# First wave of a fused attention-and-gMLP kernel: z2 of blocks 0 and 1 from centred x, the scale inside the gelu, the normed blocks through DMA transposes

## The chip, the cores and the metric

The kernel runs on one core of a Trainium2 chip. A core has a matrix engine (PE), a vector engine (DVE), an activation engine (ACT), a general engine (POOL) and a queue engine (SP) that here only issues DMAs. They run side by side and wait for each other through semaphores. The metric is device time in microseconds (us). Before the change it is 233.32 us, the median of 4 runs that lie between 233.18 and 233.46.

## The reference

x has 2048 rows (tokens) of 512 columns in bfloat16. The output is x, plus a dilated local attention of the normed x (A), plus a gated MLP of the normed x (B). Cut to what matters here:

```python
def _layernorm(x, axis=-1, eps=1e-05):
    m = jnp.mean(x, axis=axis, keepdims=True)
    v = jnp.var(x, axis=axis, keepdims=True)
    return (x - m) / jnp.sqrt(v + eps)
...
def _A_ref(x, wqkv, wo):              # 32 heads of 16, window 8, dilation 2
    qkv = ... x @ wqkv ...
    ...
    return (attention over 8 keys each) @ wo
def _B_ref(x, w_in, w_sp, b_sp, w_out):
    z = _gelu(jnp.einsum('bsd,df->bsf', x, w_in))     # 512 -> 1792
    z1 = z[..., :Fh].copy()                           # Fh = 896
    z2 = _layernorm(z[..., Fh:], axis=-1)
    g = jnp.einsum('ts,bsf->btf', w_sp, z2) + b_sp[None, :, None]
    return jnp.einsum('bsf,fd->bsd', z1 * g, w_out)
x = A_x
xn = _layernorm(x, axis=-1)
return x + _A_ref(xn, A_wqkv, A_wo) + _B_ref(xn, B_w_in, B_w_sp, B_b_sp, B_w_out)
```

## The kernel before

The 2048 rows are cut into 16 blocks of 128 rows. Everything is written as tasks with named inputs and outputs; a planner (`Plan`, L15) gives each engine one fixed order of its tasks before the program is built, from its own estimates, and puts in the semaphore waits. Some orders are written out by hand: `pe_seq` (most PE tasks stay in the order in which they are written), `dv` (the vector tasks of the first wave), a sequence of ACT tasks and one of SP loads (L734 to L739). When any task changes, the planner orders everything again, to the end of the kernel.

What happens, in order:

- **First wave** (`first_wave`, L659), blocks 0 to 3. Block b of x is loaded (L599). DVE takes its statistics (`bn`, L663) and mean and variance (`ag`, L667), POOL makes rstd, one over the root of the variance (L669), and DVE writes the normed block, (x - mean) * rstd (`nm`, L673). For block 0 this is done in two halves of 256 columns. PE transposes the block by four matmuls with the identity (`xt`, L682), ACT copies the transposed block out of PSUM into `xnT` (L688, and L700 for the two halves of block 0; DVE does it for block 3, L728). With `xnT` as the stationary operand PE multiplies by the second half of w_in (`z2_mm`, L911): per block two halves of 448 columns, each summed over four chunks dc of the 512 input columns, so 8 matmuls a block. For blocks 0 and 1 each half is cut in two tasks, chunks (0, 1) and chunks (2, 3). ACT writes gelu of the result to `z2`, with a running sum of it (L919).
- Before the first block is there, PE runs matmuls on constants (`warm`, 10 of 512 columns, L634), and one more (`fill0`) between the transposes of block 0 and block 1.
- **Wave j** (j = 0 to 3): Q and K of four blocks (L786), the products q*k on DVE (L812), their sums over a head on PE (L825, called red), V (L766), z2 of the next four blocks (L911), the layernorm of z2 (L952 squares, L958 to L974). From block 4 on the normed block does not go through PE: SP issues a DMA transpose from `xn` to `xnT` (L755).
- **z1** (L941), then the product with w_sp by a Strassen-like scheme of seven products (L1134), attention output (L1202, L1211), and the output product (L1253).

The w_in half for z2 is loaded in four chunks of 224 KB (L608): SP issues chunks 0 and 2, ACT chunks 1 and 3. Blocks 0 and 2 of x come from SP, blocks 1 and 3 from ACT. SP then issues Q weights and K weights (L620, 512 KB each), blocks 4 to 7 of x (L599), V weights (L627), blocks 8 to 11, and after these the DMA transposes of blocks 4 and up. x has eight slots; block 8 takes the slot of block 0.

The order on PE in the first wave is: warm; transposes of block 0, first half and second half; fill0; transposes of block 1; the z2 matmuls of chunks (0, 1) of blocks 0 and 1 (8 of them); chunks (2, 3) of block 0 (4); transposes of block 2; chunks (2, 3) of block 1 (4); transposes of block 3; z2 of blocks 2 and 3 (16); then Q and K of wave 0.

Of the kernel before, what the change touches and what calls it, by code (L numbers as in the profile page):

```python
# [14 lines left out]
class Plan:  # L15
# [287 lines left out]
BF = mybir.dt.bfloat16  # L303
F32 = mybir.dt.float32
ALU = mybir.AluOpType
# [9 lines left out]
    tmap=1,  # L315
    xdma=4,
    fill=1,
    warm=10,
    fill0=1,
    acc=1,  # L320
    first_plain=0,
# [3 lines left out]
def build_kernel(nc, A_x, A_wqkv, A_wo, B_x, B_w_in, B_w_sp, B_b_sp, B_w_out, out, report=False, sched_kw=None,  # L325
# [73 lines left out]
    with ExitStack() as es:  # L399
# [11 lines left out]
        def A(name, n, o2_=0):  # L411
            return ar[:, off[name] + o2_: off[name] + o2_ + n]
# [7 lines left out]
        def Fv(name, n, o2_=0):  # L420
            return fp[:, foff[name] + o2_: foff[name] + o2_ + n]
# [12 lines left out]
        def R1(key, name, n, o_=0):  # L434
            R(key, "sb", [(off[name] + o_, off[name] + o_ + n)])
# [24 lines left out]
        for s_ in range(4):  # L460
            R1(("xin", s_), "xin", 512, 512 * s_)
            if s_ < 2:
                R1(("xn0", s_), "xn", 256, 256 * s_)
            R1(("xin", 4 + s_), "xin2", 512, 512 * s_)
            R1(("xn", s_), "xn", 512, 512 * s_)
            R1(("Vn", s_), "Vn", 512, 512 * s_)
# [20 lines left out]
            R(("wk", c), "sb", [(off["wqk"] + 1024 * dc + 512 + 128 * c, off["wqk"] + 1024 * dc + 512 + 128 * c + 128)  # L487
                                for dc in range(4)])
        R1("wv_raw", "wv_raw", 2048)
        R("xnT0a", "sb", [(off["xnT"] + dc * S, off["xnT"] + dc * S + 128) for dc in range(2)])  # L490
        R("xnT0b", "sb", [(off["xnT"] + dc * S, off["xnT"] + dc * S + 128) for dc in range(2, 4)])
        for b in range(NB):
            R(("xnT", b), "sb", [(off["xnT"] + dc * S + 128 * b, off["xnT"] + dc * S + 128 * b + 128)
                                 for dc in range(4)])
# [30 lines left out]
        def T(eng, fn, **kw):  # L525
            t = plan.add(eng, fn, **kw)
            if eng == "pe" and not t.name.startswith(("warm", "fill", "xTr", "red")):
                pe_seq.append(t)
            return t
# [95 lines left out]
        for b in range(4, min(8, NB)):  # L625
# [1 line left out]
        dma("sp", lambda e: e.dma_start(A("wv_raw", 2048).rearrange("p (c n) -> p c n", c=4),  # L627
                                        A_wqkv[:, 1024:1536].rearrange("(c p) n -> p c n", p=128)),
            512 * 512 * 2, "wv", writes=["wv_raw"], name="ldwv")
        def filler(n, name, est, prio=None, reads=()):  # L630
            def warm(t):
                last = None
                for i in range(n):
                    last = t.matmul(ps[:, 3584: 4096], nc.const_aps.tensor(1.0, [128, 128], BF),  # L634
                                    nc.const_aps.tensor(1.0, [128, 512], BF), start=True, stop=True)
                return last
            T("pe", warm, reads=reads, writes=[("ps", 7)], est=est, name=name, prio=prio)

# [8 lines left out]
        def next_bank():  # L647
            k = ring[0]
            ring[0] = (k + 1) % NR
            return k  # L650
# [8 lines left out]
        def first_wave():  # L659
            dv = []  # L660

            def bn(b):
                dv.append(T("dve", lambda v: v.bn_stats(Fv("st6", 6, 9 * b), A("xin", 512, 512 * b)), reads=[("xin", b)],  # L663
                            writes=[("st6", b)], est=690, name="bnst%d" % b))

            def ag(b):
                dv.append(T("dve", lambda v: v.bn_aggr(Fv("mv", 2, 2 * b), Fv("st6", 9, 9 * b)), reads=[("st6", b), "st_eps"],  # L667
                            writes=[("mv", b)], est=200, name="bnag%d" % b))
                T("pool", lambda g: g.tensor_tensor(Fv("rstd", 1, b), Fv("mv", 1, 2 * b + 1), Fv("mhalf", 1), ALU.pow),  # L669
                  reads=[("mv", b), "mhalf"], writes=[("rstd", b)], est=580, name="rstd%d" % b)  # L670

            def nm(b, c0=0, n=512, wr=None, tag=""):
                dv.append(T("dve", lambda v: v.tensor_scalar(A("xn", n, 512 * b + c0), A("xin", n, 512 * b + c0), Fv("mv", 1, 2 * b),  # L673
                                                             Fv("rstd", 1, b), ALU.subtract, ALU.mult),
                            reads=[("xin", b), ("mv", b), ("rstd", b)],
                            writes=[wr or ("xn", b)], est=150 + n / 2, name="norm%d%s" % (b, tag)))

            def xt(b, k, dcs, rd, tag=""):
                def tr(t):
                    last = None  # L680
                    for dc in dcs:
                        last = t.matmul(ps[:, 512 * k + 128 * dc: 512 * k + 128 * dc + 128],  # L682
                                        A("xn", 128, 512 * b + 128 * dc), ident, start=True, stop=True)
                    return last
                T("pe", tr, reads=[rd, "ident"], writes=[("ps", k)], est=len(dcs) * c_mm(128), name="xt%d%s" % (b, tag))

            def ev(b, k):
                T("act", lambda a: a.activation(AC(off["xnT"] + 128 * b, [[S, 4], [1, 128]]),  # L688
                                                bank(k).rearrange("p (c n) -> p c n", c=4), ACTF.Copy),
                  reads=[("ps", k)], writes=[("xnT", b)], est=c_act(512), name="xTe%d" % b)  # L690

            bn(0)
            ag(0)
            bn(1)
            ag(1)
            k0, k1 = next_bank(), next_bank()
            for h in range(2):
                nm(0, 256 * h, 256, ("xn0", h), "ab"[h])
                xt(0, (k0, k1)[h], (2 * h, 2 * h + 1), ("xn0", h), "ab"[h])
                T("act", (lambda h: lambda a: a.activation(  # L700
                    AC(off["xnT"] + 2 * S * h, [[S, 2], [1, 128]]),
                    ps[:, 512 * (k0, k1)[h] + 256 * h: 512 * (k0, k1)[h] + 256 * h + 256].rearrange("p (c n) -> p c n", c=2),
                    ACTF.Copy))(h),
                  reads=[("ps", (k0, k1)[h])], writes=["xnT0" + "ab"[h]], est=c_act(256), name="xTe0" + "ab"[h])
            filler(cfg["fill0"], "fill0", 216.0 * cfg["fill0"], reads=(("xn0", 1),))
            nm(1)
            k = next_bank()
            xt(1, k, range(4), ("xn", 1))
            ev(1, k)
            bn(2)  # L710
            ag(2)
            bn(3)
            nm(2)
            ag(3)
            nm(3)
            u = [(b, hf, next_bank()) for b in range(2) for hf in range(2)]
            for b, hf, k in u:
                z2_mm(b, hf, k, (0, 1))
            for b, hf, k in u:
                if b == 1 and hf == 0:  # L720
                    k2 = next_bank()
                    xt(2, k2, range(4), ("xn", 2))
                    ev(2, k2)
                z2_mm(b, hf, k, (2, 3))
                z2_gelu(b, hf, k)
            k = next_bank()
            xt(3, k, range(4), ("xn", 3))
            dv.append(T("dve", (lambda k: lambda v: v.tensor_copy(  # L728
                AC(off["xnT"] + 128 * 3, [[S, 4], [1, 128]]), bank(k).rearrange("p (c n) -> p c n", c=4)))(k),
                reads=[("ps", k)], writes=[("xnT", 3)], est=c_dve(512), name="xTe3"))  # L730
            for b in (2, 3):
                z2_half(b, 0)
                z2_half(b, 1)
            plan.sequence(dv)  # L734
            sq = {t.name: t for t in plan.tasks if t.name.startswith("ld")}
            plan.sequence([sq[n] for n in ("ldq", "ldk", "ldx4", "ldx5", "ldx6", "ldx7", "ldwv")])
            names = ["xTe0a", "xTe0b", "xTe1", "z2g0_0", "xTe2", "z2g0_1", "z2g1_0"]
            named = {t.name: t for t in plan.tasks if t.name in names}
            plan.sequence([named[n] for n in names])  # L739
# [167 lines left out]
        def z2_mm(b, hf, k, dcs=range(4)):  # L907
            def mm(t):
                last = None
                for dc in dcs:  # L910
                    last = t.matmul(ps[:, 512 * k: 512 * k + HF], AC(off["xnT"] + dc * S + 128 * b, [[1, 128]]),  # L911
                                    AC(off["w_in2"] + FH * dc + HF * hf, [[1, HF]]), start=(dc == 0), stop=(dc == 3))
                return last
            rd = "xnT0" + "ab"[dcs[0] // 2] if b == 0 else ("xnT", b)
            T("pe", mm, reads=[rd] + [("w_in2", dc) for dc in dcs], writes=[("ps", k)],
              est=len(dcs) * c_mm(HF), name="z2_%d_%d_%d" % (b, hf, dcs[0]))

        def z2_gelu(b, hf, k):
            T("act", lambda a: a.activation(  # L919
                A("z2", HF, FH * b + HF * hf), ps[:, 512 * k: 512 * k + HF], ACTF.Gelu_apprx_tanh,  # L920
                accum_out=Fv("s1", 1, 2 * b + hf)),
              reads=[("ps", k)], writes=[("z2h", b, hf), ("s1", b, hf)], est=c_act(HF, accum=True),
              name="z2g%d_%d" % (b, hf), tbl="gelu")

        def z2_half(b, hf):
# [475 lines left out]
```

## Time and profile before

| what | value |
|---|---|
| median of 4 runs | 233.32 us (233.18 to 233.46) |
| the profiled execution | 233.59 us, of it a span of 231.7 us |
| PE busy | 226.7 us of the span |
| DVE busy | 205.0 us |
| ACT busy | 128.6 us |
| POOL busy | 40.8 us |
| DMA queue of SP (q1) | 59.1% of 16 DMA engines' time |

The span runs from the first to the last instruction; the 1.9 us around it are start and end of the execution. Clock times below (such as "at 8.02") are us from the start of the span. Busy PE time is modelled for the end of each matmul, so start-to-start distances are used for its pace. A few matmul records are missing from the trace.

### The profile page before, as it was taken

Reading aid. Unit: us, or ns where it says so; the run is one execution under the profiler, and the core shown is the slowest. Engines: PE = TensorE matmul, PEld = TensorE weight load, DVE = VectorE, ACT = ScalarE, POOL = GpSimd, SP = SyncE. Lnnn points to the kernel's source line nnn. Section 1 sums busy time; section 2 is a strip of 40 time slices with the busy share of each in tenths; the row PEclk is TensorE's granted clock in tenths of the full one; section 3 lists DMA queues with packets and bytes.
Section 4 is the critical chain, followed back from the end, with each engine's and each line's share of the span. In section 5 each row is a group of like instructions: output and inputs, shape, how many; then the busy total and the mean of one; then the engine's idle time right before and its main releaser. Section 6 shows DMA issues by size and latency. Waiting matters only on the chain.

```text
span 231.7 us, 3288 instructions
## 1 busy us (share of the span) xinstructions
PE 226.7 (98%) x1222; PEld 111.6 (48%) x1238; DVE 205.0 (88%) x235; ACT 128.6 (56%) x235; POOL 40.8 (18%) x74
## 2 busy tenths in 40 slices
PE   8999999999999999999999999999999999999995
PEld 2444445444434565555555454454545444545442
DVE  4688996998998899999999999999999999979910
ACT  2698758975899997556562243333423433255321
POOL 4456838197007101000000000000000000000000
DMA  6974999783107300449609999999999647745162
GB/s 201 336 213 100 206 269 317 129 250 117 34 16 166 106 3 0 99 82 219 215 9 185 235 208 250 254 214 256 278 314 180 166 167 139 260 103 112 44 151 68
DMA packets 76800, 38.65 MB, mean 167 GB/s; under 512 B 65132, under 2 KB 75244, under 8 KB 75760
## 3 DMA queue, kind: packets, MB, share of 16 engines
q1 hardware_dynamic: 70400, 31.63, 59.1%
q10 hardware_dynamic: 5568, 4.69, 7.1%
q0 software_dynamic: 816, 2.12, 3.0%
q8 instruction: 10, 0.16, 0.3%
q14 instruction: 6, 0.05, 0.1%
HBM read 18.49 MB, written 4.21 MB: 98 GB/s over the span
## 4 chain that ended last, share of the span: by engine, by line
PE 94%; DMA 3%; issue 1%; ACTq 1%; DVE 0%; ACT 0%
PE ps L1134 37%; PE ps L1253 16%; PE ps L786 12%; PE ps L941 11%; PE ps L911 10%; PE ps L766 6%; PE ps L825 3%; DMA arena<-in_A_x_dram 3%; ACTq L608 0%; PE ps L682 0%; DVE fpool L663 0%; ACTq L599 0%; DVE arena L673 0%; ACT arena L1095 0%
## 5 line engine op out<-in xcount | busy, mean ns | idle before, releaser
L1134 PE MATMUL ps<-arena 128*128 128x448 bf16 x448 | 90.6, 352 | 0.0
L1134 PEld LDWEIGHTS ps<-arena 128*128 128x128 bf16 x448 | 43.8, 98 | 42.8 <-ACT arena L1095 0.3
L1253 PE MATMUL ps<-arena 128*128 128x512 bf16 (+2 forms) x178 | 42.1, 366 | 0.5
L1202 DVE TENSOR_TENSOR arena<-arena 128x4096 bf16<-128x4096 bf16 x16 | 36.6, 2287 | 0.2
L812 DVE TENSOR_TENSOR arena<-arena 128x4096 bf16<-128x4096 bf16 x16 | 36.3, 2281 | 0.0
L1211 DVE TENSOR_TENSOR arena<-arena 128x4096 bf16<-128x4096 bf16 (+2 forms) x24 | 33.7, 1402 | 1.1 <-DMA arena<-arena 0.3
L1095 ACT ACTIVATE arena<-ps 128x512 bf16<-128x512 f32 (+2 forms) x23 | 13.0, 564 | 34.4 <-PE ps L1134 24.0
L786 PE MATMUL ps<-arena 128*128 128x512 bf16 x124 | 27.9, 379 | 0.3 <-issue 0.2
L1253 PEld LDWEIGHTS ps<-arena 128*128 128x128 bf16 x187 | 17.9, 98 | 18.5
L911 PE MATMUL ps<-arena 128*128 128x448 bf16 x128 | 25.5, 353 | 0.0
L941 PE MATMUL ps<-arena 128*128 128x448 bf16 x128 | 24.8, 353 | 0.0
L1027 DVE TENSOR_TENSOR arena<-arena 128x1024 bf16<-128x1024 bf16 x32 | 21.0, 686 | 0.9 <-DMA arena<-in_B_w_sp_dram 0.6
L919 ACT ACTIVATE arena<-ps 128x448 bf16<-128x448 f32 x32 | 17.2, 547 | 4.8 <-PE ps L911 2.9
L786 PEld LDWEIGHTS ps<-arena 128*128 128x128 bf16 x128 | 12.3, 98 | 15.5 <-issue 1.3
L941 PEld LDWEIGHTS ps<-arena 128*128 128x128 bf16 x128 | 14.4, 114 | 10.2 <-issue 0.8
L947 ACT ACTIVATE arena<-ps 128x896 bf16<-128x896 f32 x16 | 14.4, 916 | 8.7 <-PE ps L941 8.7
L794 ACT ACTIVATE arena<-ps 128x1024 bf16<-128x1024 f32 x16 | 16.3, 1019 | 4.8 <-PE ps L786 4.3
L911 PEld LDWEIGHTS ps<-arena 128*128 128x128 bf16 x128 | 12.2, 98 | 11.7 <-issue 0.4
L952 ACT ACTIVATE arena<-arena 128x896 bf16<-128x896 bf16 x16 | 15.1, 945 | 0.1
L766 PE MATMUL ps<-arena 128*128 128x512 bf16 x61 | 14.1, 379 | 0.4 <-issue 0.3
L1143 ACT ACTIVATE ps<-ps,fpool 128x448 f32<-128x448 f32 x16 | 9.7, 605 | 8.2 <-PE ps L1134 8.2
L1095 ACT ACTIVATE ps<-arena 128x512 f32<-128x512 bf16 (+2 forms) x17 | 9.7, 574 | 6.4 <-ACT arena L1095 4.7
(70 smaller groups left out, 196.2 us busy)
## 6 DMA issues: line engine op xcount, KB each, us to landing
arena<-vscr SPq DMA_DIRECT2D x8, 1152.0 KB, 6.4
arena<-in_A_x_dram ACTq DMA_DIRECT2D x18, 128.0 KB, 4.1
vscr<-arena POOLq DMA_DIRECT2D x16, 128.0 KB, 3.5
arena<-in_A_x_dram SPq DMA_DIRECT2D x14, 128.0 KB, 5.4
out_dram<-arena ACTq DMA_DIRECT2D x14, 128.0 KB, 2.6
arena<-in_A_wqkv_dram SPq DMA_DIRECT2D x3, 512.0 KB, 6.2
arena<-in_B_w_in_dram SPq DMA_DIRECT2D x1, 896.0 KB, 5.0
arena<-in_B_w_out_dram SPq DMA_DIRECT2D x1, 896.0 KB, 6.2
```

The source lines that it names most:

```text
L766: last = t.matmul(bank(k), AC(off["xnT"] + dc * S + 128 * b, [[1, 128]]), AC(off["wv_raw"] + 512 * dc, [[1, 512]]), start=(dc == 0), stop= ...
L786: last = t.matmul(bank(k + which), AC(off["wqk"] + 1024 * dc + col0, [[1, 128]]), AC(off["xnT"] + dc * S + 512 * j, [[1, 512]]), start=(dc ...
L812: T("dve", lambda v: v.tensor_tensor(pbv, qb, kb, ALU.mult), reads=rd, writes=[("pb", s_)], est=c_dve(4096, 2.0), name="prod%d_%d" % (j, c ...
L911: last = t.matmul(ps[:, 512 * k: 512 * k + HF], AC(off["xnT"] + dc * S + 128 * b, [[1, 128]]), AC(off["w_in2"] + FH * dc + HF * hf, [[1, H ...
L919: T("act", lambda a: a.activation(A("z2", HF, FH * b + HF * hf), ps[:, 512 * k: 512 * k + HF], ACTF.Gelu_apprx_tanh, accum_out=Fv("s1", 1, ...
L941: last = t.matmul(ps[:, 512 * (k + hf): 512 * (k + hf) + HF], AC(off["xnT"] + dc * S + t0, [[ts, 128]]), AC(off["w_in1"] + FH * dc + HF * ...
L1027: T("dve", (lambda o_, x_, y_: lambda v: v.tensor_tensor(o_, x_, y_, ALU.subtract))(o_, x_, y_), reads=rd, writes=[wr], est=c_dve(NK * 128 ...
L1095: T("act", lambda a: a.activation(out_, in_, ACTF.Copy), reads=reads, writes=writes, est=c_act(n), name=name)
L1134: last = t.matmul(half(bk), lh(k), rh(k), start=(new and k == 0), stop=(k == NK - 1), skip_group_check=True)
L1202: T("dve", (lambda tv, iv, av: lambda v: v.tensor_tensor(tv, iv, av, ALU.mult))(tv, iv, av), reads=[("attn", j)] + ([("Ve", par)] if q < 2 ...
L1211: T("dve", (lambda o_, n: lambda v: v.tensor_tensor(o_, two(0, n), two(n, n), ALU.add))(o_, n), reads=[] if n > 512 else ["Vs", ("Ve", par ...
L1253: last = t.matmul(po, lh, rh, start=False, stop=(q == len(order) - 1), skip_group_check=True)
```

## The change

In words:

- For blocks 0 and 1 DVE writes x - mean (`ce`, without rstd) to a scratch place in `pb`, block 0 in two halves. PE transposes these centred blocks, ACT copies them to a new place `XCT`, and the z2 matmuls of blocks 0 and 1 read that place. The factor rstd, one number a row, is given to the gelu of these two blocks as its scale.
- The normed blocks 0 and 1 are still needed for Q, K, V and z1. DVE writes them as before (`nm`, now whole blocks), after the centred ones, and SP issues a DMA transpose for each (`xd`) into `xnT`.
- SP's order becomes: Q weights, K weights, transpose of block 0, block 8 of x, transpose of block 1, blocks 4 to 7, V weights, blocks 9 to 11, transposes of block 4 and up (with block 12 ahead of the transpose of block 7).
- `warm` goes from 10 to 8 matmuls, `fill0` from 512 to 256 columns.
- The statistics of block 1 follow the centring of block 0. DVE's order in the first wave becomes: statistics 0, centre 0 (two halves), statistics 1, centre 1, norm 0, statistics 2, norm 1, statistics 3 and norm 2, norm 3.
- PE's order in the first wave becomes: warm; transposes of block 0 (two halves); fill0; block 0, first half of columns, chunks (0, 1) (2 matmuls); transposes of block 1; block 0, second half, chunks (0, 1) (2); block 0, first half, chunks (2, 3) (2); block 1, chunks (0, 1) (4); block 0, second half, chunks (2, 3) (2); transposes of block 2; block 1, chunks (2, 3) (4); transposes of block 3; z2 of blocks 2 and 3; Q and K.
- The planner's new order further on differs in places: statistics of block 8 stand ahead of those of block 4 on DVE; each group of reds stands one PE task later than before (the first one three tasks later); the product of wave 3, pair 1 stands behind the softmax subtraction of wave 2 and the z2 layernorm of wave 3 on DVE.

The diff, cut to its core:

```diff
-    warm=10,
+    warm=8,
...
+        R1("xc1", "pb", 512, 512)
+        XCT = off["pb"] + 1024
...
+            def ce(b, c0, n, wr, tag=""):
+                dv.append(T("dve", lambda v: v.tensor_scalar(A("pb", n, 512 * b + c0), A("xin", n, 512 * b + c0),
+                                                             Fv("mv", 1, 2 * b), None, ALU.subtract),
+                            reads=[("xin", b), ("mv", b)], writes=[wr], est=150 + n / 2, name="cent%d%s" % (b, tag)))
+
+            def xd(b):
+                dma("sp", lambda e: e.dma_start_transpose(AC(off["xnT"] + 128 * b, [[S, 4], [1, 128]]),
+                                                          A("xn", 512, 512 * b)),
+                    128 * 512 * 2, ("xT", b), reads=[("xn", b)], writes=[("xnT", b)], name="xTd%d" % b, xbar=True)
...
             bn(0)
             ag(0)
+            k0, k1 = next_bank(), next_bank()
+            for h in range(2):
+                ce(0, 256 * h, 256, ("xc0", h), "ab"[h])
+                xt(0, (k0, k1)[h], (2 * h, 2 * h + 1), ("xc0", h), "ab"[h])
...
+            filler(cfg["fill0"], "fill0", 216.0 * cfg["fill0"], reads=(("xc0", 1),), w=256)
             bn(1)
             ag(1)
...
+            ce(1, 0, 512, "xc1")
+            nm(0)
             bn(2)
             ag(2)
+            nm(1)
             bn(3)
             nm(2)
             ag(3)
             nm(3)
+            for b in range(2):
+                xd(b)
+            kx = next_bank()
             u = [(b, hf, next_bank()) for b in range(2) for hf in range(2)]
...
+            z2_mm(*u[0], (0, 1))
+            xt(1, kx, range(4), "xc1")
...
+            z2_mm(*u[1], (0, 1))
+            z2_mm(*u[0], (2, 3))
+            z2_gelu(*u[0])
+            z2_mm(*u[2], (0, 1))
+            z2_mm(*u[3], (0, 1))
+            z2_mm(*u[1], (2, 3))
+            z2_gelu(*u[1])
+            k2 = next_bank()
+            xt(2, k2, range(4), ("xn", 2))
+            ev(2, k2)
+            for b, hf, k in u[2:]:
                 z2_mm(b, hf, k, (2, 3))
                 z2_gelu(b, hf, k)
...
-            plan.sequence([sq[n] for n in ("ldq", "ldk", "ldx4", "ldx5", "ldx6", "ldx7", "ldwv")])
+            plan.sequence([sq[n] for n in ("ldq", "ldk", "xTd0", "xTd1", "ldx4", "ldx5", "ldx6", "ldx7", "ldwv")])
...
+                    xo = XCT + dc * 256 + 128 * b if b < 2 else off["xnT"] + dc * S + 128 * b
+                    last = t.matmul(ps[:, 512 * k: 512 * k + HF], AC(xo, [[1, 128]]),
                                     AC(off["w_in2"] + FH * dc + HF * hf, [[1, HF]]), start=(dc == 0), stop=(dc == 3))
...
             T("act", lambda a: a.activation(
                 A("z2", HF, FH * b + HF * hf), ps[:, 512 * k: 512 * k + HF], ACTF.Gelu_apprx_tanh,
+                scale=Fv("rstd", 1, b) if b < 2 else 1.0,
                 accum_out=Fv("s1", 1, 2 * b + hf)),
```

## The prediction

> **What bounds the kernel now.** I read the page first, then the chain that ended last in order of time, then the timelines of PE, DVE and SP over the first 24 us.
>
> ```profile
> span 231.7 us, 3288 instructions
> ...
> PE 226.7 (98%) x1222; PEld 111.6 (48%) x1238; DVE 205.0 (88%) x235; ACT 128.6 (56%) x235; POOL 40.8 (18%) x74
> ...
> PE 94%; DMA 3%; issue 1%; ACTq 1%; DVE 0%; ACT 0%
> ```
>
> PE is the bound: 98% busy and 94% of the chain. The rest of the chain is DMA, and the chain in order of time shows which:
>
> ```profile
> 2.21 5.95 DMA arena<-in_A_x_dram
> 8.16 0.02 issue
> 8.19 0.69 DVE fpool L663
> 8.88 0.32 DVE arena L673
> 9.21 0.05 issue
> 9.25 0.40 PE ps L682 x4
> 9.65 0.76 PE ps L911 x4
> 10.41 0.03 issue
> 10.43 0.40 PE ps L682 x4
> 10.83 3.03 PE ps L911 x16
> ```
>
> The load issued at 2.21 on ACT is block 3 of x. It lands at 8.16; its statistics, norm and transposes follow, and from 10.43 on PE never stands still: over 14 to 215 us the list of PE's waits holds 0.5 us, all "issue" beside missing records. So the end of the kernel is 10.43 plus PE work that the change leaves as it is. The PE timeline up to there:
>
> ```profile
> 5.49 0.57 PE L682 MATMUL ps<-arena 128*128 128x128 bf16 x4 [0.22 <-DVE arena L673]
> 5.90 0.38 PE L634 MATMUL ps<-const-bfloat16-1.0 128*128 128x512 bf16 x1
> 6.36 0.40 PE L682 MATMUL ps<-arena 128*128 128x128 bf16 x4
> 6.59 2.54 PE L911 MATMUL ps<-arena 128*128 128x448 bf16 x12
> 9.25 0.40 PE L682 MATMUL ps<-arena 128*128 128x128 bf16 x4
> 9.49 0.92 PE L911 MATMUL ps<-arena 128*128 128x448 bf16 x4
> 10.43 0.40 PE L682 MATMUL ps<-arena 128*128 128x128 bf16 x4
> ```
>
> Read starts, since ends are modelled. A z2 matmul takes 0.19 us (0.76 / 4 in the chain), four transposes 0.24 (10.43 to 10.67). Twelve z2 matmuls from 6.59, with a stop of 0.1 at 7.35 for the copy of block 1 (ACT 6.79 + 0.60), end at 8.97; PE then idles 0.28 until the norm of block 2 lets it go at 9.25, and 0.19 more before 10.43. PE is already early here: it waits for DVE, and DVE for x:
>
> ```profile
> 6.99 0.69 DVE L663 BATCH_NORM_STATS2 fpool<-arena 128x6 f32<-128x512 bf16 x1 [0.69 <-DMA arena<-in_A_x_dram]
> 8.19 0.69 DVE L663 BATCH_NORM_STATS2 fpool<-arena 128x6 f32<-128x512 bf16 x1 [0.27 <-DMA arena<-in_A_x_dram]
> 9.96 0.41 DVE L673 TENSOR_SCALAR arena<-arena,fpool 128x512 bf16<-128x512 bf16 x1 [0.66 <-POOL fpool L669]
> ```
>
> **The start of block 0.** Statistics 0 end at 4.40. Norm 0 started at 5.11, behind statistics 1 and rstd 0; the centring needs neither and starts at about 4.44, so the first transpose moves from 5.49 to 4.44 + 0.38 = 4.82, 0.67 earlier. Subtracting alone is not in the trace; the nearest rows, the norm of 256 columns (0.33) and of 512 (0.41), price it, and nothing at all below. Two constant matmuls fewer (each 0.42: the ten end at 5.27) end the warm-up at about 4.4, so they don't delay it.
>
> **Where the 0.67 goes.** Block 1 is centred behind centre 0 and statistics 1: 4.44 + 0.58 (two halves) + 0.65 + 0.2 give 5.9 with the hand-overs, where norm 1 stood before (5.89). Its transposes stay at 6.36, its copy at 7.39. Until then PE has four z2 matmuls of block 0, done by 7.0. The next in its order are chunks (2, 3) of block 0, which need chunk 2 of w_in: issued at 2.18 and 5.8 to landing in the DMA view, 7.97. Before, PE filled this time with block 1 and came to these chunks at 8.02, just after the landing. Now it idles from 7.0 to 8.02 and has 2 + 4 + 2 = 8 matmuls ahead of the transposes of block 2, not 4: 8.02 + 8 x 0.19 = 9.54 (norm 2 is ready at 9.21), + 0.24 + 4 x 0.19 = 10.54 for the transposes of block 3, against 10.43. The whole gain is lost in the wait for w_in, and **0.1 us** is added. The bound below is 0: norm 3 is done at 9.96 + 0.41 = 10.37, tied to a load whose rivals in the queues do not change before 8.16. Above: PE before could take 0.47 (0.28 + 0.19) of a later w_in chunk, and now none, so a chunk 0.3 later would cost 0.4.
>
> **Norms 0 and 1 on DVE**, 2 x 0.41, fall into its waits for x: norm 0 at 6.2 to 6.65, before 6.99; norm 1 at 7.83 (after the mean of block 2, 7.72 + 0.11), the next instruction 0.33 later at 8.16, before 8.19. Cost 0; if statistics 3 slipped, norm 3 and PE would slip by as much. rstd 0 and 1 on POOL are done by 6.5, before either use.
>
> **The gelu with a row scale** (4 of 32): without scale L919 takes 0.54; with a per-row operand, the L1143 copies of the same size take 0.605. 4 x 0.06 at most on ACT, which at 11.6 and later stays over 0.5 us ahead of the PE tasks that reuse its PSUM banks. Cost 0.
>
> **SP, with all that it now issues.**
>
> ```profile
> 5.45 1.99 SPq L599 DMA_DIRECT2D arena<-in_A_x_dram  x4
> 7.48 0.48 SPq L627 DMA_DIRECT2D arena<-in_A_wqkv_dram  x1
> 13.76 9.15 SPq L755 DMA_TRANSPOSE arena<-arena  x7
> ```
>
> Transpose 0 waits on SP for norm 0 (6.7), and a transpose takes SP 1.27; then block 8 (0.45), transpose 1 from 8.4 to 9.7, blocks 4 to 7 from 9.7 (before 5.45), V weights 11.7, blocks 9 to 11, transposes of block 4 on. The queue moves in order: K weights, issued at 4.90, land 6.2 later at 11.1; blocks 4 to 7 then came 0.37 apart (11.5 to 12.6). A transpose moves as many bytes as such a load, 0.37, or takes at most what is left of its quiet 2.5 to landing after 1.27 of issue, 1.2. So transpose 1 lands between 11.1 + 3 x 0.37 = 12.2 and 11.1 + 1.2 + 0.37 + 1.2 = 13.9. Q of wave 0 needs it at 13.7 + 0.1 = 13.8. I take the middle, 13.0: no stall, hidden behind the z2 matmuls of blocks 2 and 3; past them each us costs one. Four transposes issued from 31.64 to 41 behind larger loads took 7.2 to 11.3 to landing: that would be 15.6 to 19.7, 1.8 to 5.9 late. They stood behind 2.3 MB and beside POOL's stores, and nothing like it runs at 11 us, so those rows are far.
>
> Blocks 4 to 7 land at 13.1 to 14.3, 1.6 later; the transpose of block 7, issued at 17.70 before, goes out near 19.6 and lands near 22, and Q of wave 1 starts at 24.1. V weights land near 15.7 and are used at 20.6. Covered by 2 us and more; with that gone, PE would wait for DVE's norms.
>
> **DVE further on** starts wave 1 1.5 late and has 0.7 more work. Its waits take that up: 0.94 at 72.67, 0.58 at 76.36 (for w_sp), over 2 us between 33 and 42. Its tightest hand-overs to PE were 0.6 to 0.8 us (softmax subtraction, 91.70 + 1.22, to the reds at 93.51; the product at 99.15 + 2.28 to 102.18), and those reds now stand one z1 group (0.76) later. Cost 0; if 1.5 came through whole, 1.5 - 0.7 = 0.8.
>
> **Sum.** +0.1 on 231.7, 231.8; on the profiled 233.59, 233.7. That execution is 0.27 above the median, so the median goes from 233.32 to **233.4**.
>
> **The clock, bounded from rows.** PE starts at half pace: constant matmuls 0.42 apart for 512 columns, later 0.216. The windows' granted clock says 1.00 throughout, so only the distances show it. Full pace came between 5.06 and 5.49, 4.2 to 4.65 after the first matmul, in unbroken work. Now PE rests 0.4 to 0.6 us before 4.82, 0.25 before 5.75 and up to 1 us before 8.02. If a rest restarts the count, full pace comes at 4.82 + 4.65 = 9.5 or 8.02 + 4.65 = 12.7, and the half-pace work after 8.02 costs (9.5 - 8.02) / 2 = 0.7 to 4.65 / 2 = 2.3. I take 0: in the stretch that ended in full pace before, part of a rest of 0.4 may already have lain.
>
> The Trainium skill speaks against the change here: "TensorE: Matmul & The Clock Gate", Part 1, says that full clock needs a busy window of about 3.4 us whose phase is not tied to the kernel. Eight constant matmuls at 0.42 are 3.4 us, so by that page hardly any phase leaves a window without a rest; were windows with a rest refused, each would cost half of 3.4, an estimate of 1.7 us. No row here shows how much rest a window bears.
>
> **Rivals.**
> - *The clock stays low* (PE, 4.8 to 12.7): for it the new rests, against it the four runs before, 0.28 us apart. 0.7 to 2.3, middle 1.5: **234.9**. It decides once half pace lasts beyond 8.02.
> - *Q of wave 0 waits for transpose 1*: decides from a landing after 13.8, each us is one us; with 15.6, **235.2**.
> - *DVE comes late to the reds* at 94 to 103: 0.8, **234.2**.
> - *The early start is carried to the end*, as it would be were PE bound by its own work from 5.49: 233.32 - 0.67 = **232.65**. PE's 98% speaks for it, the chain through the load of x against it.
>
> **How the numbers follow.** Forecast 0.52, clock 0.17, transposes 0.11, DVE 0.10, early start 0.10. Faster or slower is told from no change at 0.2%, 0.47 us. Same: 0.47 of the forecast and 0.01 of the transposes, 0.48. Slower: 0.05 + 0.17 + 0.10 + 0.10 = 0.42. Faster: 0.10. The forecast's own range is 233.2 to 233.8. For 8 in 10 the range must reach over most of the clock's and transposes' cases: 232.9 to 235.5 leaves out the early start and about 0.08 above.
>
> **What would show it.** First transposes at 4.8; PE idle from 7.0 to 8.0; transposes of block 3 at 10.5; Q at 13.8 without a wait; no PE waits later. Wrong if z2 matmuls after 8.02 are 0.37 apart (clock), if Q starts after 14, if L825 waits for DVE, or if the transposes of block 3 start before 10.3.

## The result, and the profile after

The changed kernel takes 233.74 us, the median of 37 executions (233.12 to 235.98); the kernel before, timed beside it, 233.25 us (56 executions, 232.82 to 233.83). The ratio is 1.0027, with a 95% interval of 1.0019 to 1.0035: slower by half a microsecond in the median and by 0.63 in the mean (233.91 against 233.28), which the ratio follows; that is a little more than the 0.2% that can be told from no change. Beside the median the upper end has moved: 8 of the 37 executions lie above 234.2, none of the 56 before.

The profiled execution took 233.8 us, with a span of 231.18 (231.74 before). Its 2.62 us around the span are unusual; the other profiled executions of this study have 1.84 to 2.01. Span, busy time and the chain, from the page of the kernel after:

```profile
span 231.2 us, 3295 instructions
...
PE 225.4 (98%) x1220; PEld 111.4 (48%) x1236; DVE 206.4 (89%) x237; ACT 129.1 (56%) x235; POOL 40.2 (17%) x74
...
PE 95%; DMA 2%; issue 1%; SPq 1%; ACT 0%
```

The chain of the kernel after in order of time (start, us, what):

```profile
2.18 5.03 DMA arena<-in_B_w_in_dram
7.21 0.05 issue
7.26 1.69 PE ps L935 x8
8.95 0.22 PE ps L694 x4
9.17 0.76 PE ps L935 x4
9.93 0.22 PE ps L694 x4
10.15 3.03 PE ps L935 x16
```

The load in the chain is no longer block 3 of x but chunk 2 of w_in, issued at 2.18 on SP, landed at 7.21. From there PE is bound by itself: eight z2 matmuls, transposes of block 2, four matmuls, transposes of block 3. The PE timeline of the kernel after:

```profile
0.84 3.57 PE L637 MATMUL ps<-const-bfloat16-1.0 128*128 128x512 bf16 x8 [0.84 <-PEq L1411]
4.49 0.48 PE L694 MATMUL ps<-arena 128*128 128x128 bf16 x4
4.80 0.27 PE L637 MATMUL ps<-const-bfloat16-1.0 128*128 128x256 bf16 x1
5.75 0.54 PE L935 MATMUL ps<-arena 128*128 128x448 bf16 x2 [0.67 <-DMA arena<-in_B_w_in_dram]
6.12 0.39 PE L694 MATMUL ps<-arena 128*128 128x128 bf16 x4
6.34 0.54 PE L935 MATMUL ps<-arena 128*128 128x448 bf16 x2
7.26 1.69 PE L935 MATMUL ps<-arena 128*128 128x448 bf16 x8 [0.37 <-DMA arena<-in_B_w_in_dram]
...
9.76 0.39 PE L694 MATMUL ps<-arena 128*128 128x128 bf16 x4
```

The transposes of block 0 start 1.00 earlier than before (4.49, not 5.49; 0.28 of it because block 0 landed earlier, at 3.16 and not 3.44), yet PE gives it back in two waits for w_in, chunk 1 (landed 5.61) and chunk 2. The time from chunk 2's matmuls to the transposes of block 3, 9.76 - 7.26 = 2.50, is what matters: the prediction had 2.52.

That the transposes of block 3 start at 9.76 here and at 10.43 in the profile before is no gain of the change. In this execution the loads happened to land early: block 3 at 7.41, before at 8.16. With the loads of the execution before (chunk 2 at 7.96) the same work gives 7.96 + 0.05 + 2.50 = 10.51.

Two sums help to read all that follows. From the transposes of block 3 to the last matmul PE takes 218.7 us before (229.13 - 10.43 = 218.70) and after (228.45 - 9.76 = 218.69), and the span ends 221.3 us (before) or 221.4 us (after) behind these transposes. So an execution's span tells when its block 3 was transposed, unless PE waits later. Over all executions the median span is 231.3 before (35 executions of one batch) and 231.8 after (37), which is 10.0 and 10.4 for the transposes of block 3.

The wait for chunk 2 alone does not explain this. Chunk 2 and block 3 land together: in the twelve profiled executions that keep the order of the first loads, chunk 2 came 0.17 to 0.26 ahead of block 3. By the old chain the transposes of block 3 start 2.27 behind the landing of block 3 (10.43 - 8.16). In the four profiled executions in which PE takes up chunk 2 within 0.14 of its landing and at full pace, they start 2.29 to 2.45 behind it (the profile after 9.76 - 7.41 = 2.35, twelve constants 2.29, and the two runs with the K weights moved 2.43 and 2.45). So in executions like these the new chain costs 0.02 to 0.18 over the old, however late the two loads come. The rest of the half microsecond must lie in the pace of PE or in a later wait, unless the first loads land later with the change; the profiles do not show that they do (block 3 at 7.11 to 8.10 with it, 7.42 to 8.16 without).

### The profile page after: what moved, and what is told of

It reads as the page before. It is cut to its first block, busy times and chain, and to the rows that moved or that the text cites. A ratio compares the mean times of both kernels' runs of the same rounds, so it can differ in the third digit from the quotient of the medians.

```text
span 231.2 us, 3295 instructions
## 1 busy us (share of the span) xinstructions
PE 225.4 (98%) x1220; PEld 111.4 (48%) x1236; DVE 206.4 (89%) x237; ACT 129.1 (56%) x235; POOL 40.2 (17%) x74
## 4 chain that ended last, share of the span: by engine, by line
PE 95%; DMA 2%; issue 1%; SPq 1%; ACT 0%
PE ps L1159 37%; PE ps L1278 16%; PE ps L809 12%; PE ps L966 11%; PE ps L935 10%; PE ps L789 6%; PE ps L848 3%; DMA arena<-in_B_w_in_dram 2%; SPq L602 0%; PE ps L694 0%; SPq L611 0%; ACT arena L1120 0%
## 5 line engine op out<-in xcount | busy, mean ns | idle before, releaser
L835 DVE TENSOR_TENSOR arena<-arena 128x4096 bf16<-128x4096 bf16 x16 | 36.2, 2280 | 0.0
L809 PE MATMUL ps<-arena 128*128 128x512 bf16 x124 | 27.9, 379 | 0.3 <-issue 0.2
L809 PEld LDWEIGHTS ps<-arena 128*128 128x128 bf16 x128 | 12.4, 98 | 15.3 <-issue 0.4
L943 ACT ACTIVATE arena<-ps 128x448 bf16<-128x448 f32 x28 | 15.1, 548 | 2.0
L789 PE MATMUL ps<-arena 128*128 128x512 bf16 x61 | 14.7, 379 | 0.3 <-issue 0.2
```

The costliest lines, as they stand in the source:

```text
L789: last = t.matmul(bank(k), AC(off["xnT"] + dc * S + 128 * b, [[1, 128]]), AC(off["wv_raw"] + 512 * dc, [[1, 512]]), start=(dc == 0), stop= ...
L809: last = t.matmul(bank(k + which), AC(off["wqk"] + 1024 * dc + col0, [[1, 128]]), AC(off["xnT"] + dc * S + 512 * j, [[1, 512]]), start=(dc ...
L835: T("dve", lambda v: v.tensor_tensor(pbv, qb, kb, ALU.mult), reads=rd, writes=[("pb", s_)], est=c_dve(4096, 2.0), name="prod%d_%d" % (j, c ...
```

## The experiments

Every kernel is its parent (before or after) with the edit shown. All were timed beside the kernel before, whose median in the four batches was 233.25, 233.23, 233.23 and 233.15.

### Ten constant matmuls again, and the order of block 1

The change cut the constant matmuls from 10 to 8 and reordered the z2 matmuls around chunk 2 of w_in. The first experiments undo one, the other, and both.

```diff
-    warm=8,
+    warm=10,
```

> The changed kernel with ten constant matmuls again. Clock theory: the two matmuls that were taken away left a rest on PE before 4.8 in which the full pace is not granted in some executions; with them back the long upper tail (up to 235.98) goes and the ratio to before falls from 1.0027 to about 1.0005. Theory of the wait for w_in (chunks (2, 3) of block 0 stand ahead of block 1's chunks): PE rests from 7.0 to the landing either way, so ratio and tail stay, 1.002 to 1.003.

Measured: 233.45 us (12 executions, 232.91 to 234.09), ratio 1.0009 [0.9997, 1.0021]. The executions above 234.2 are gone and the median has moved down by 0.29 of the 0.49.

```diff
             z2_mm(*u[1], (0, 1))
-            z2_mm(*u[0], (2, 3))
-            z2_gelu(*u[0])
             z2_mm(*u[2], (0, 1))
             z2_mm(*u[3], (0, 1))
+            z2_mm(*u[0], (2, 3))
+            z2_gelu(*u[0])
             z2_mm(*u[1], (2, 3))
```

> The changed kernel with block 1's chunks (0, 1) again ahead of block 0's chunks (2, 3). w_in theory: four matmuls (0.76 us) less stand behind the landing of chunk 2, so a late landing is absorbed as before; ratio 1.000 to 1.0005 and a spread like that of before (1 us). Clock theory: no change, ratio 1.002 to 1.003 and the tail stays.

Measured: 233.57 (233.04 to 234.92), ratio 1.0021 [1.0004, 1.0037]. The long upper end stays (234.18, 234.74, 234.92). In the profiled execution the transposes of block 3 waited for DVE and started at 10.23, with block 3 of x landed at 7.96: 2.27 behind the landing, as before the change (10.43 - 8.16). So this order puts the old chain back, and still the interval of the ratio lies above 1.

Both edits together:

> Both edits. If one theory holds alone, equal to the better of the two single edits; if both hold, each single edit is at about 1.001 and this one at 1.000. If neither, 1.0027, and the cause lies elsewhere, in the DMA transposes or later on DVE.

Measured: 233.68 (233.28 to 234.54), ratio 1.0021 [1.0009, 1.0032]. This is not better than either alone, and none of the theories said so. Three of its twelve executions lie above 234.2 (234.35 twice, and 234.54), although it has ten constant matmuls. The profiled execution had full pace by 5.05 and its transposes of block 3 at 10.27, again 2.27 behind the landing of block 3 (8.00). The intervals of the three runs overlap; what lies between them is not resolved.

### The kernel before, with fewer constant matmuls

```diff
-    warm=10,
+    warm=8,
```

> The kernel before with eight constant matmuls, nothing else; PE then rests about 1.1 us before the first transposes at 5.49. Clock theory: slower than before with a long upper tail, ratio 1.002 or more. w_in theory: no change, ratio 1.000, since PE waits for x in any case.

Measured: 234.29 (233.04 to 234.83), ratio 1.0033 [1.0016, 1.0049]. Nothing but the two constant matmuls differs from the kernel before; every engine's order is the same. The times fall in two groups: five executions at 233.04 to 233.85, as before, and seven at 234.25 to 234.83. The one that was profiled is of the lower group (233.16):

```profile
0.84 3.57 PE L634 MATMUL ps<-const-bfloat16-1.0 128*128 128x512 bf16 x8 [0.84 <-PEq L1386]
5.38 0.54 PE L682 MATMUL ps<-arena 128*128 128x128 bf16 x4 [0.97 <-DVE arena L673]
```

PE rests 0.97 behind the eight constants, and its first transposes already run at full pace (0.07 from one to the next; at half pace they are 0.11 apart). So this rest does not always cost the pace, and the pace of the seven executions above 234.2 was not seen. The two matmuls carry no data that anything reads, so what they change can only be the time and the pace of PE. To see the pace, four instead of eight:

```diff
-    warm=10,
+    warm=4,
```

> The kernel before with 4 constant matmuls at the start instead of 10, nothing else changed. Clock theory: as with 8, and more often: most executions at 234.3 or above, none or few at 233.3, with z2 matmuls 0.37 apart for a stretch after 8 us in the trace of one. Rival (the loss with 8 had another cause than the pace, such as the planner's order): within 0.3 of 233.25, or as with 8 (234.3) with matmuls at full pace in the trace.

Measured: 234.77 (5 executions, 234.43 to 235.13), ratio 1.0069 [1.0053, 1.0084]. No execution is left in the lower group. Its PE timeline:

```profile
0.84 1.86 PE L634 MATMUL ps<-const-bfloat16-1.0 128*128 128x512 bf16 x4 [0.84 <-PEq L1386]
5.17 0.65 PE L682 MATMUL ps<-arena 128*128 128x128 bf16 x4 [2.47 <-DVE arena L673]
5.62 0.63 PE L634 MATMUL ps<-const-bfloat16-1.0 128*128 128x512 bf16 x1
6.04 0.63 PE L682 MATMUL ps<-arena 128*128 128x128 bf16 x4
6.47 4.65 PE L911 MATMUL ps<-arena 128*128 128x448 bf16 x12
10.95 0.40 PE L682 MATMUL ps<-arena 128*128 128x128 bf16 x4
11.19 0.92 PE L911 MATMUL ps<-arena 128*128 128x448 bf16 x4
11.94 0.39 PE L682 MATMUL ps<-arena 128*128 128x128 bf16 x4
```

The twelve z2 matmuls from 6.47 to 10.95 are 0.373 apart, the four and sixteen after them 0.19; before, the same twelve took 2.54 instead of 4.65. All the data was there (chunk 2 of w_in landed at 7.23, block 3 of x at 7.42). With 7.42 + 2.3 the transposes of block 3 would have stood at 9.7; they stand at 11.94. The clock's own column does not show this. The windows of the same kernel (stretch and its length, then the busy time and number of instructions of PE, weight loads, DVE, ACT and POOL, the granted clock, DMA share, GB/s):

```profile
7.50:9.50 2.00, 2.00 (x7) 0.80 (x6) 1.34 (x4) 0.00 (x0) 1.14 (x3) 1.00 1.09 383
11.00:13.00 2.00, 2.00 (x18) 1.27 (x17) 0.63 (x2) 1.70 (x7) 0.81 (x6) 1.00 1.11 349
```

PE is fully busy in both stretches and the clock reads 1.00 in both, but the first holds 7 matmuls in 2 us and the second 18 (some of them shorter). Only the distances tell.

### The kernel after, with four and with twelve

```diff
-    warm=8,
+    warm=4,
```

> The kernel after with 4 constant matmuls of 512 columns at the start instead of 8, so that the matrix engine rests about 2 us before the first transposes. Clock theory (full pace needs some 4 us of nearly unbroken matmuls, and what is left of a window after a rest doesn't count): half pace now lasts into the z2 matmuls behind chunk 2 of w_in in nearly all executions; the z2 matmuls after about 7.3 to 8 us are 0.37 us apart instead of 0.19 for 1 to 4 us; median 234.6 to 236, most executions over 234.3. Rival (the constant matmuls only fill time, and the 0.5 us of the change come from the order around w_in and block 1): z2 matmuls 0.19 apart after 8 us, median 233.7 within 0.3.

Measured: 234.87 (6 executions, 233.61 to 235.49), ratio 1.0067 [1.0045, 1.0089]. The PE timeline:

```profile
4.76 0.58 PE L694 MATMUL ps<-arena 128*128 128x128 bf16 x4 [2.05 <-DVE arena L681]
...
8.05 2.43 PE L935 MATMUL ps<-arena 128*128 128x448 bf16 x8 [0.33 <-DMA arena<-in_B_w_in_dram]
10.32 0.39 PE L694 MATMUL ps<-arena 128*128 128x128 bf16 x4
10.54 0.92 PE L935 MATMUL ps<-arena 128*128 128x448 bf16 x4
11.30 0.39 PE L694 MATMUL ps<-arena 128*128 128x128 bf16 x4
```

The eight z2 matmuls behind chunk 2 take 10.32 - 8.05 = 2.27, not 1.52 as at 7.26 in the profile after: one 0.33, three 0.37 and one 0.25 from the next, then 0.19. Here the late pace costs 0.75, straight on the chain, since chunk 2 had landed at 7.92.

```diff
-    warm=8,
+    warm=12,
```

> The kernel after with 12 constant matmuls instead of 8. They end at about 5.3 to 5.5, 0.5 to 0.7 after the first centred half is ready, so the transposes of block 0 move there, but the matrix engine has a rest of up to 1 us before chunk 2 of w_in that takes this up. Clock theory: full pace in every execution by about 5.5, nothing above 234.1, median 233.2 to 233.45, like 10 or better. Rival (the matrix engine's own work in the first 8 us bounds the end): 0.3 to 0.5 above the run with 10.

Measured: 233.29 (12 executions, 232.91 to 234.07), ratio 1.0005 [0.9992, 1.0017]: like before, and the transposes of block 0 are 1.33 later than in the profile after (5.82, not 4.49). That is the plainest sign that the early start is worth nothing here. The slowest of the twelve, 234.07, was the profiled one, and shows something else:

```profile
5.82 0.39 PE L694 MATMUL ps<-arena 128*128 128x128 bf16 x4
...
10.27 0.39 PE L694 MATMUL ps<-arena 128*128 128x128 bf16 x4
10.50 3.19 PE L935 MATMUL ps<-arena 128*128 128x448 bf16 x16
14.28 1.89 PE L809 MATMUL ps<-arena 128*128 128x512 bf16 x8 [0.59 <-DMA arena<-arena]
```

Q of wave 0 (L809) waits 0.59 for a DMA transpose. In this execution the K weights landed at 12.51 (10.64 in the profile after), transpose 0 at 13.09, block 8 at 13.60 and transpose 1 at 13.93, one behind the other in SP's queue. So the rival "Q waits for transpose 1" is real, in executions whose weights land late. Such late weights cannot be brought about at will, so the next two runs tried to make Q independent of them.

### The K weights behind the transposes

After planning, the load of the K weights is moved on SP behind transpose 1; all other orders are kept.

```diff
         plan.schedule(**(sched_kw or {}))
+        o = plan.order["sp"]
+        o.remove(by_name["ldk"])
+        o.insert(o.index(by_name["xTd1"]) + 1, by_name["ldk"])
```

With 8 constant matmuls:

> The kernel after, with the load of the K weights moved on SP from ahead of the transpose of block 0 to behind the transpose of block 1; all other orders kept. The two transposes then wait in the queue only for the Q weights. Transpose theory (part of the slow tail of after is Q of wave 0 waiting for transpose 1 when the K weights land late, as in the profiled execution with 12 constant matmuls: K at 12.51, transpose 1 at 13.93, Q at 14.28): transpose 1 lands at 10.5 to 12, Q never waits, nothing above 234.5 unless the clock does it, median 233.4 to 233.6. Clock theory alone (all of the tail is late full pace): the tail to 234.5 to 235.5 stays, with a median of 233.7 as before this edit.

Measured: 234.31 (6 executions, 233.45 to 235.01), ratio 1.0047 [1.0030, 1.0064]. With 10:

> As the run before, with 10 constant matmuls instead of 8, so that both suspected causes are gone. Both theories together: no tail, highest 233.7 or less, median 233.0 to 233.25, 0.2 to 0.45 below the run with 10 alone (233.45). If the K weights were not a cause: 233.45 with times up to 234.1 as with 10 alone. If the later K weights or blocks 4 to 7 (about 0.5 us later) are missed by K of wave 0 or the statistics of wave 1: 233.7 or above, with a wait of the matrix engine behind 16.7 us.

Measured: 234.45 (6 executions, 234.11 to 235.47), ratio 1.0063 [1.0048, 1.0078]: a full microsecond worse than ten constant matmuls alone, where the theory said better. Transpose 1 did come early (10.95 and 11.19) and Q of wave 0 did not wait. But the third possibility of the expectation holds. Blocks 4 to 7, now behind the K weights, landed at 14.13 to 16.05 with 8 and at 14.52 to 17.65 with 10 (12.43 to 13.53 in the profile after), and the waits after 12 us of the run with 10 are new or longer (the third was 0.2 in the profile after; engine and line, waited for: us in total, times, longest):

```profile
ACT arena L793 <- DMA arena<-arena: 2.4, 1, 2.4
...
DVE arena L775 <- DMA arena<-arena: 1.5, 1, 1.5
...
PE ps L809 <- issue: 0.9, 1, 0.9
...
PE ps L848 <- DVE arena L835: 0.7, 1, 0.7
```

PE stands 0.9 before Q of wave 1, which starts at 24.89; the transpose of block 7 had landed at 24.80 (21.54 in the profile after). It stands 0.7 before reds (L848, at 44.08) that wait for the product on DVE (L835). The second wait is of the kind of the rival "DVE comes late to the reds", though at 44 and not at 94 to 103. Blocks 4 to 7, 2 to 4 us later than in the profile after, are the likely cause of both. The edit traded one wait for two larger ones and shows how little cover there is behind the forecast's "covered". The profiled execution with 8 (233.87) has no such wait; what its slower executions waited for was not seen.

### Twelve, and block 8 behind block 7

If lateness in SP's queue is what is left, block 8 of x, which the change loads between the two transposes, is the cheapest thing to move.

```diff
-    warm=8,
+    warm=12,
...
         plan.schedule(**(sched_kw or {}))
+        for e, n, after in (("sp", "ldx8", "ldx7"), ("dve", "bnst8", "bnst7")):
+            o = plan.order[e]
+            o.remove(by_name[n])
+            o.insert(o.index(by_name[after]) + 1, by_name[n])
```

> The kernel after with 12 constant matmuls, and with block 8 of x loaded behind block 7 instead of between the two transposes, its statistics on the vector engine moved behind those of block 7; all other orders kept. Queue theory (what is left above before with 12 constant matmuls is the later landing of transpose 1 and of blocks 4 to 7 behind block 8, in executions whose Q and K weights land late): transpose 1 and blocks 4 to 7 land about 0.35 to 0.5 earlier than with block 8 between, median 233.0 to 233.2, highest 233.7 or less, no slower than before. Rival (block 8's place costs nothing, and the scatter has another cause): 233.3 with times up to 234, as with 12 alone.

Measured: 233.69 (9 executions, 233.12 to 233.86), ratio 1.0020 [1.0010, 1.0030]. The queue theory falls: the median did not come down. Transpose 1 landed at 12.10 in the profiled execution and PE never waited for it. What that execution shows is a plain price of twelve constant matmuls:

```profile
0.84 5.26 PE L637 MATMUL ps<-const-bfloat16-1.0 128*128 128x512 bf16 x12 [0.84 <-PEq L1415]
5.91 0.41 PE L694 MATMUL ps<-arena 128*128 128x128 bf16 x4
...
7.37 2.16 PE L935 MATMUL ps<-arena 128*128 128x448 bf16 x10
...
10.35 0.39 PE L694 MATMUL ps<-arena 128*128 128x128 bf16 x4
```

The constants hold PE until 5.9, and from there its own work, with stops of 0.34 and 0.09, takes 4.44 to the transposes of block 3. Chunk 2 of w_in had landed at 7.53, so with fewer constants 7.53 + 0.05 + 2.50 = 10.08 would have been possible, 0.27 earlier. In the execution with twelve above, the constants cost nothing of this kind: chunk 2 landed at 7.72, and 7.72 + 0.05 + 2.50 = 10.27 is where its transposes of block 3 stand. Why this run is 0.4 above the one with twelve alone is not shown; the two ran on different chips.

### Loading block 3 earlier, before the change

The chain before goes through block 3 of x, the last of the first loads on ACT's queue. Two runs issue it ahead of chunk 3 of w_in in the kernel before; in the first the planner orders the later work anew, in the second every other order is kept.

```diff
-        ld_win2(3, "act")
-        ld_win2(2, "sp")
         ld_x(3, "act")
+        ld_win2(2, "sp")
+        ld_win2(3, "act")
```

> The kernel before with one change: on the activation engine's queue, block 3 of x is issued ahead of chunk 3 of w_in (SP's chunk 2 keeps its place). Theory (the chain before goes through the load of block 3, and the matrix engine is early by 0.28 + 0.19 us): block 3 lands near 7.4, norm 2 and norm 3 come some 0.4 earlier, the transposes of block 3 start at about 10.0 instead of 10.43: 232.9, 0.3 to 0.45 below before. Rival (w_in bounds the first wave as much as x does): chunk 3 lands 0.3 or more after 8.0 and takes the gain: 233.2 to 233.4.

The second run moves block 3 after planning:

```diff
         plan.schedule(**(sched_kw or {}))
+        o = plan.order["act"]
+        o.remove(by_name["ldx3"])
+        o.insert(o.index(by_name["ldw_in2_3"]), by_name["ldx3"])
```

> The kernel before, with block 3 of x issued ahead of chunk 3 of w_in on the activation engine's queue and every other order kept as in before (the earlier run of this swap let the planner order the later work anew). Theory (block 3 bounds the first wave): transposes of block 3 start at 9.6 to 10.0 and the median is 0.2 to 0.5 below before. Rival (the earlier run's 0.2 below before was the new later order, or chance): within 0.1 of before.

Measured: 233.03 (12 executions, 232.69 to 233.60), ratio 0.9993 [0.9981, 1.0005], and 233.22 (11 executions, 232.98 to 233.56), ratio 0.9997 [0.9988, 1.0005]. Block 3 landed at 6.56 and 6.29 and its transposes started at 9.63 and 9.96, PE being bound almost wholly by its own work from the transposes of block 0 on (4.45 in both). Of the expected 0.3 to 0.45 the runs show 0.2 at most, and neither is told from no change. In the second the list of waits has a new one, 0.2 of the reds (L825) for the softmax subtraction on DVE (L845). No version of this study is shown to beat the kernel before.

## Why the prediction was right, and where it was not

The forecast was 233.4, with 232.9 to 235.5 as its range; measured were 233.74. The range held. The likeliest case had +0.1 and the runs have about +0.5, so the outcome lies in the "slower" that had 0.42 rather than in the "same" that had 0.48. That it fell inside the range is owed to the room left for the rivals; the sum behind 233.4 does not give the 0.5. One of the prediction's own signs of being wrong also came: the transposes of block 3 started before 10.3 in the profile, at 9.76. The sign took the landing of chunk 2 as fixed at 7.97, and here it was 7.21.

- **What bounds the kernel.** Right. With the loads of each execution in hand, its end follows from the start of block 3's transposes: 221.3 to 221.4 to the end of the span in all profiled executions without a later wait.
- **The start of block 0.** Right in size. Block 0 to first transposes took 5.49 - 3.44 = 2.05 before and 4.49 - 3.16 = 1.33 after, 0.72 less; the step said 0.67.
- **Where the 0.67 goes.** Right in mechanism: lost in the wait for chunk 2, then eight matmuls instead of four ahead of block 2. Chunk 2 to block 3 took 2.50 as computed. Against the old chain that costs 0.02 to 0.18, as worked out above. Not foreseen was the wait for chunk 1, 0.67 before 5.75, which cost nothing because the one for chunk 2 follows it. The +0.1 agrees with the run of ten constant matmuls, 233.45, which is +0.20 with an interval from -0.07 to +0.49; the order alone was never resolved, and putting block 1 first didn't lower the time beyond the intervals.
- **Norms 0 and 1 on DVE.** Right: they ran at 5.80 and 6.94, and the statistics of block 3 started at 7.43, 0.02 behind the landing.
- **The gelu with a row scale.** Mis-sized: 0.63 to 0.64 against 0.54 to 0.57 without scale, some 0.09 and not 0.06 at most; no one waited for it.

The ACT timeline of the kernel after has both forms:

```profile
10.92 0.64 ACT L943 ACTIVATE arena<-ps,fpool 128x448 bf16<-128x448 f32 x1
...
11.53 0.56 ACT L943 ACTIVATE arena<-ps 128x448 bf16<-128x448 f32 x1
```

- **SP and the transposes.** "No stall" held in the profile after, where transpose 1 landed at 12.01, 1.37 behind the K weights, against 1.9 taken. It failed in one profiled execution by 0.59, for a cause that the step took as fixed: the K weights came at 10.62 to 12.51 over the profiled executions, not always at 11.1.
- **DVE further on.** Right for the kernel after, with no wait of PE behind 14 us. The cover was smaller than "2 us and more" made it sound: blocks 4 to 7 later by 2 to 4 us, and PE waited 0.9 and 0.7.
- **The clock.** This is the term that was mis-sized: "I take 0". The argument for 0 was that the stretch which ended in full pace before may already have held part of a rest of 0.4. The runs show instead that in the kernel before ten constant matmuls were enough and eight were not: eight put seven of twelve executions 1.0 to 1.6 us above its median, and four put all of them 1.2 to 1.9 above. The trace with four shows matmuls at half pace until 10.95 and nothing else late. In the kernel after, four cost 1.1 over eight. The prediction also took full pace as coming 4.2 to 4.65 after the first matmul. The profile before shows only that it came after 4.63 and by 5.49; over the profiled executions with ten constants it came as early as 3.75 and as late as 6.33 to 6.55, which is 2.9 to 5.7 after the first matmul.

How much of the 0.49 in the kernel after is the clock is not settled. For it speaks that the long upper end goes when ten constants are put back into the kernel after, that two constants fewer alone cost as much in the kernel before (+0.33%) as the whole change (+0.27%), that the wait for chunk 2 is too small (0.02 to 0.18), and the bound 0.7 to 2.3 of the rival, into which the two traces with four constants fall: 0.75 and 11.94 - 9.7 = 2.2. Against a full account: the intervals of the two ratios, with eight and with ten, overlap; the run with both edits has ten constants too, and three of twelve executions above 234.2, which no theory here explains; no execution of the kernel after with eight constants and late pace fell to the profiler (in the one profiled full pace came by 4.49, with block 1 first by 5.6, with the K weights moved by 6.2, all before chunk 2); and late weights lengthen some executions too. What is shown is that the clock lengthens executions where constants are taken away; that it makes most of the long ones of the kernel after is the likeliest reading, not a measured share.

The Trainium skill had spoken against the change here ("TensorE: Matmul & The Clock Gate", Part 1: a busy window of about 3.4 us, whose phase is not tied to the kernel). The traces agree in kind. After a rest of 2 us or more, unbroken work took 5.8 us to full pace in one execution (5.17 to 10.95) and, with short rests, between 4.7 and 5.0 in another (4.76 to 9.5 or 9.75), which lies between one and two such windows; and executions of one program differ. Full pace, once reached, outlasted rests of 0.93 us (ten constants, block 3 loaded early) and 1.11 us (eight, K weights moved), so the prediction's case of 12.7, in which the rest before chunk 2 restarts the count, did not occur in any profile. How much rest is borne before full pace is reached no run here measured.

## What to carry to other kernels

Dummy matmuls at the start are not slack to be trimmed when the first real work comes earlier: count them as time at which the clock is earned, and after a change look at the distance of matmuls, and at the upper end of the times, not at the median of a few runs alone. An earlier start is worth what the next load allows: follow each operand's landing before a gain at the front is carried to the end. And a cover read from one profile is worth no more than the loads' scatter between executions, here a microsecond and more.

## What was not expected of the hardware

- The same loads land at different times from one execution to the next. Over the profiled executions that keep the order of the first loads, block 3 of x landed between 7.11 and 8.16 and the K weights (where they directly follow the Q weights) between 10.62 and 12.51. In the runs with the K weights behind the transposes, block 6 landed 2.35 us behind block 5 in one execution and 0.36 in the other.
- The moment at which PE reaches full pace scatters as widely: from 3.75 and from 4.15 on in the two executions with ten constant matmuls and block 3 loaded early, after 4.63 and by 5.49 in the profile before, and between 6.33 and 6.55 in the kernel after with ten constants and the K weights moved.
- The time around the span is 1.8 to 2.1 in nearly all executions, but 2.3 to 2.8 in a few (2.62 in the profiled one of the kernel after). The cause is not known.
